# Attention, experts and FFN on one core: last tokens' products in float32, one addition on ScalarE, loads reordered

## The chip, the cores and the metric

One of the eight cores of a Trainium2 chip runs the whole kernel. The metric is the device time in microseconds (us); less is better. The trace names the engines PE (TensorE's matmuls), PEld (its weight loads), DVE (VectorE), ACT (ScalarE), POOL (GpSimd) and SP (the queue that issues most DMAs).

## The reference

Three layers follow one another on 2 sequences of 544 tokens (32 global, 512 local), 8 heads of 64:

```python
out_g = softmax(scale * q_g @ k_all.T) @ v_all            # global tokens see all
out_l = softmax(where(|i - j| <= 32, scale * q_l @ k_l.T, -1e9) ++ scale * q_l @ k_g.T) @ v   # local: window and globals
x = tokens(out)                                           # 1088 x 512
e = argmax(x @ w_gate); gate = softmax(...)[e]             # one of 8 experts per token
# each expert takes its first `capacity` = 288 tokens, in the tokens' order
y = relu(disp @ w1[e]) @ w2[e]                             # 512 -> 1024 -> 512
x = gate * y
h = x @ w_in; g = clip-like(h); out = g @ w_out            # 512 -> 2048 -> 512
```

Every softmax divides by its sum plus 1e-9.

## The kernel before, in words

The order of every engine is written out by hand; the engines run their instructions in that order and wait on semaphores.

**Attention** runs in 16 steps `k` (2 sequences x 2 pairs of token tiles x 4 pairs of heads). In the round of step `k` the program issues `exps(k+1)` (ScalarE), `scores(k+2)` (TensorE, then VectorE adds the mask, L313), the items of `first[k]`, `transp(k)` and its evacuation `evac_t(k)` (ScalarE and VectorE), `av(k-1)` (TensorE) with its evacuation by VectorE (L356), and the items of `plan[k]`. The four groups of global queries go through `glob1`, `glob1b`, `glob2`, `glob3`, one a step, beginning at steps 0, 3, 5 and 8. In PSUM the banks of kind "V" rotate, and `glob1` holds two of them until `glob1b`.

**Routing** of a pair of token tiles is put into three steps by `route(k, b, tp)`: at `k` the logits, `recips` (add 1e-9 to the sums of the softmax, then the reciprocal, both VectorE, L507 and L508) and `choose` (argmax and one-hot, L536); at `k+1` `slots` (each token's place in its expert, and the running counts `racc`) and the first `x_rows` (the token turned back to rows, scaled by the reciprocal); `scatter` puts the rows into the DRAM tensor `xd` by an indirect DMA of GpSimd. Routed steps are 7, 10 and 13; the last pair is routed behind step 15.

**Weights** of the experts come in chunks of 128x1024. `weight_load` issues the DMA on SP; `weight_h` (ScalarE, L218) writes the rounded half H; `weight_l` (L230) writes the rest L = raw - H. Products are taken as three of `float32r` (H x, L x, H x_low). The first eight chunks (units 0 and 1, expert 0) are loaded at steps 2 to 9, cast on ScalarE at steps 5 to 12, and their L's are GpSimd's. Raw buffers number four until the attention's memory is given up, then eight.

**The last two tiles** of tokens don't go through DRAM: `xt0` is loaded from `xd` once the earlier scatters have landed, and the last rows are added to it by a product with a matrix `place` that has a one at each token's slot. Their rows are split into halves first (L723 on ScalarE, L729 on VectorE), so that the products are five sets of four (L739). The sum is split again and is the first input of expert 0.

**The experts** follow: `expert_tile` runs 48 matmuls of 512 columns for up to 128 tokens; `rest` runs again for the tokens above 128 and above 256. The jobs in `todo` cast the next expert's chunks between them, one or two at each call of `bg` (ScalarE, every eighth on VectorE, L220), and take their L's on VectorE at the next call. Then comes the FFN.

Of the kernel before, what the change touches and what calls it, by code (L numbers as in the profile page):

```python
# [19 lines left out]
WARM_0, WARM_1, WARM_2, WARM_3, WARM_4 = 9, 5, 3, 2, 0  # L20
# [8 lines left out]
def tile_attention_moe_ffn(  # L29
# [97 lines left out]
    def load_values(u):  # L127
        b, hp = divmod(u, NHP)
        VT[u] = at.tile([P, 5, P], F32, tag="vt", name=f"vt{u}", bufs=NBU)
        nc.sync.dma_start(VT[u], vx[b, hp])  # L130
        if hp % 2 == 1:
            QG[u // 2] = at.tile([P, 4 * SG], F32, tag="qgt", name=f"qgt{u}", bufs=4)
            nc.sync.dma_start(QG[u // 2], qg[b, hp // 2])
# [29 lines left out]
    half = const.tile([P, 1], F32, name="half")  # L163
    racc = const.tile([P, E], BF16, name="racc")
# [29 lines left out]
    def raw_tile(name):  # L194
        n = nraw[0]
        nraw[0] += 1
        if more_raw and n % 8 >= 4:
            return more_raw[0].tile([P, 1024], F32, tag="raw2", name=name, bufs=4)
# [341 lines left out]
    def slots(b, lo, hi):  # L540
# [3 lines left out]
        for i in range(lo, hi):  # L544
# [11 lines left out]
            op=ALU.mult)  # L556
        rs = rt.tile([P, E], F32, tag="rs", name=f"rs{b}{lo}", bufs=1)
        nc.vector.tensor_reduce(out=rs, in_=OH[b][:, lo:hi, :].rearrange("p i e -> p e i"), op=ALU.add, axis=AX.X)
        with nc.allow_low_precision(reason="whole numbers, one of the terms not zero"):
            nc.vector.tensor_reduce(out=sidx[:, ts], in_=ex[:, :n, :], op=ALU.add, axis=AX.X)  # L560
# [40 lines left out]
    def consts():  # L601
        nc.gpsimd.tensor_copy(tri_b, tri_f)
        nc.gpsimd.memset(ones_b, 1.0)
        nc.gpsimd.memset(half, 0.5)
        nc.gpsimd.memset(racc, 0.0)
# [20 lines left out]
    def keep_warm(n):  # L626
        warm = ps_a("warm")
        for _ in range(n):
            nc.tensor.matmul(warm, zero.bitcast(BF16)[:, :P], zero.bitcast(BF16)[:, :512], start=True, stop=True)
# [13 lines left out]
    load_values(5)  # L643
    wq = [(u, c) for u in range(2) for c in range(4)]
# [3 lines left out]
    for g, k in enumerate((0, 3, 5, 8)):  # L648
# [10 lines left out]
    def route(k, b, tp):  # L659
# [19 lines left out]
    for k in range(NS):  # L679
# [54 lines left out]
    for ns, k0 in ((range(5), range(KD)),):  # L734
        for n in ns:
            x, at_ = parts[n]
            for k in k0:
                ks = slice(k * P, (k + 1) * P)
                nc.tensor.matmul(px0[:, ks], x[:, ks], at_, start=n == k == 0, stop=n == 4 and k == KD - 1)  # L739
# [11 lines left out]
    nc.vector.tensor_scalar(out=cnt, in0=pc[:1, :E], scalar1=float(cap), scalar2=None, op0=ALU.min)  # L751
    actx.close()
# [218 lines left out]
    for c in range(2):  # L971
        weight_load(3, c)
    XH[0, 0] = X0
    x_load(1, 0, 1)
    for c in range(2, 4):
        weight_load(3, c)
    wl = [(2 * e + i, c) for e in range(1, E) for i in range(2) for c in range(4)]
    wn = [8]
# [17 lines left out]
    todo = [(2 * e + i, c) for e in range(1, E) for i in range(2) for c in range(4)]  # L996
# [14 lines left out]
    for e in range(E):  # L1011
# [3 lines left out]
        def bg():  # L1015
# [11 lines left out]
            for f in wide[n] if wide else ():  # L1027
                f()
            if e > 0 and small:
# [381 lines left out]
```

## Time and profile before

| | us |
|---|---|
| median of 3 runs | 467.0 |
| lowest, highest run | 464.29, 467.17 |
| profiled execution, its own time | 462.71 |
| its span, first to last instruction | 460.8 |
| PE busy | 442.3 (96%) |
| PEld busy | 372.1 (81%) |
| DVE busy | 335.2 (73%) |
| ACT busy | 242.9 (53%) |
| POOL busy | 95.8 (21%) |

The granted TensorE clock is 1.00 (of 2.4 GHz) over the whole span. A busy share is an average over stages with different limits: attention and routing take the first 91 us, the experts the time to about 254, the FFN the rest. An instruction that stalls at its start still counts as busy on its engine, so that a longer duration than usual of the same form is a wait too.

### The profile page before, as it was taken

The numbers are of one execution on the slowest core, as the hardware profiler recorded it, in microseconds if no ns is written. First come the engines' busy times: TensorE is split into PE (matmuls) and PEld (weight loads), VectorE is DVE, ScalarE is ACT, GpSimd is POOL, SyncE is SP. The second block draws the span as 40 slices with busy tenths as digits, with TensorE's granted clock in tenths as the row PEclk, the third lists the DMA queues.
The fourth block names the chain that finished last, engine by engine and source line by source line (L and its number), as shares of the span: only waits on it lengthen the run. The fifth ranks groups of instructions, "written<-read, shape, count | busy, mean of one in ns | idle before, by whom it ended". The sixth has DMA issues, their size and how long they took to land. (4 is left out here: it accounts for less than half of the span.)

```text
span 460.8 us, 8110 instructions
## 1 busy us (share of the span) xinstructions
PE 442.3 (96%) x2875; PEld 372.1 (81%) x2876; DVE 335.2 (73%) x715; ACT 242.9 (53%) x508; POOL 95.8 (21%) x98
## 2 busy tenths in 40 slices
PE   8998989999999999999999899998999999999997
PEld 4876677787577777777777799998999899999996
DVE  4787798674156389936898976787888988878633
ACT  5779666273244478726766675645444344534321
POOL 1105365300000000000001642232133131322321
PEclk9999999999999999999999999999999999999999
DMA  8999554589349169963986340653221410000203
GB/s 273 312 332 366 171 185 134 192 278 395 129 127 316 47 242 389 375 239 123 341 299 243 98 149 0 211 200 93 91 75 64 134 49 1 0 2 0 70 1 127
DMA packets 34595, 79.17 MB, mean 172 GB/s; under 512 B 3761, under 2 KB 8497, under 8 KB 34546
## 3 DMA queue, kind: packets, MB, share of 16 engines
q1 hardware_dynamic: 31698, 70.40, 44.8%
q0 software_dynamic: 1408, 4.46, 2.9%
q10 hardware_dynamic: 1440, 3.67, 2.3%
q8 instruction: 29, 0.48, 0.5%
q14 instruction: 20, 0.16, 0.1%
HBM read 63.77 MB, written 14.75 MB: 170 GB/s over the span
## 5 line engine op out<-in xcount | busy, mean ns | idle before, releaser
L1158 PE MATMUL fh<-oldH,H 128*128 128x256 f32 (+1 forms) x256 | 64.7, 328 | 2.6 <-DVE g L1176 2.1
L230 DVE TENSOR_TENSOR L<-raw,H 128x1024 fp32r<-128x1024 f32 x56 | 66.3, 1217 | 0.9 <-ACT H L218 0.6
L1198 PE MATMUL acc<-oldH,H 128*128 128x256 f32 (+2 forms) x240 | 65.1, 332 | 1.3 <-ACT H L280 0.7
L218 ACT CAST H<-raw 128x1024 fp32r<-128x1024 f32 x57 | 58.0, 1049 | 10.0 <-PEq L895 8.2
L1158 PEld LDWEIGHTS fh<-oldH,H 128*128 128x128 f32 x256 | 44.8, 189 | 6.0 <-DVE g L1176 2.5
L1184 ACT CAST oldH<-g 128x256 fp32r<-128x256 f32 (+2 forms) x36 | 17.9, 496 | 56.8 <-DVE g L1176 56.8
L1198 PE MATMUL acc<-oldH,L 128*128 128x256 f32 (+2 forms) x144 | 47.2, 328 | 0.0
L1198 PEld LDWEIGHTS acc<-oldH,H 128*128 128x128 f32 x240 | 43.3, 189 | 4.0 <-issue 1.0
L1172 DVE SCALAR_TENSOR_TENSOR r<-r 128x256 f32<-128x256 f32 (+2 forms) x48 | 31.2, 650 | 21.0 <-ACT r L1163 21.0
L1185 POOL TENSOR_TENSOR oldH<-g,oldH 128x256 fp32r<-128x256 f32 (+2 forms) x24 | 26.8, 1119 | 73.3 <-ACT oldH L1184 63.5
L1158 PE MATMUL fh<-oldH,L 128*128 128x448 f32 (+1 forms) x128 | 41.6, 325 | 0.0
L599 DVE TENSOR_TENSOR hl<-pt,hh 128x512 fp32r<-128x512 f32 (+1 forms) x24 | 15.7, 653 | 35.6 <-ACT hh L598 35.6
L860 PE MATMUL py<-H,hh 128*128 128x512 f32 (+1 forms) x96 | 38.6, 402 | 0.0
L860 PE MATMUL py<-L,hh 128*128 128x512 f32 (+1 forms) x96 | 37.6, 391 | 0.0
L285 DVE TENSOR_TENSOR L<-co,H 128x512 fp32r<-128x512 f32 x32 | 22.9, 722 | 18.4 <-ACT H L280 18.4
L1163 ACT ACTIVATE r<-fh,half 128x256 f32<-128x256 f32 (+2 forms) x48 | 27.0, 564 | 17.5 <-PE fh L1158 17.1
L845 ACT ACTIVATE hs<-ph 128x512 f32<-128x512 f32 (+1 forms) x24 | 14.4, 598 | 41.2 <-PE ph L842 41.0
L1158 PE MATMUL fh<-oldL,H 128*128 128x384 f32 x128 | 35.2, 339 | 0.2
L931 POOL DMA_INDIRECT yg_own<-yd,idx x2 | 2.3, 1135 | 147.5 <-DVE co L270 147.2
L270 DVE SCALAR_TENSOR_TENSOR co<-raw,ca 128x512 uint32<-128x512 uint32 x32 | 31.5, 992 | 0.9
L324 ACT ACTIVATE sm<-sm,ng 128x224 f32<-128x224 f32 x64 | 30.0, 476 | 3.7 <-DVE ng L313 3.7
L860 PE MATMUL py<-H,hl 128*128 128x512 f32 (+1 forms) x96 | 28.5, 401 | 0.0
(202 smaller groups left out, 1014.8 us busy)
## 6 DMA issues: line engine op xcount, KB each, us to landing
raw<-in_w_dram SPq DMA_DIRECT2D x64, 512.0 KB, 5.7
raw<-in_w_in_dram SPq DMA_DIRECT2D x14, 512.0 KB, 4.9
raw<-in_w_out_dram SPq DMA_DIRECT2D x12, 512.0 KB, 3.7
xd<-zero SPq DMA_DIRECT2D x16, 256.0 KB, 5.9
vt<-in_vx_dram SPq DMA_DIRECT2D x8, 320.0 KB, 4.8
xt<-xd SPq DMA_DIRECT2D x8, 256.0 KB, 6.5
yd<-zero SPq DMA_DIRECT2D x8, 256.0 KB, 3.7
yd<-ys SPq DMA_DIRECT2D x8, 256.0 KB, 5.6
```

The lines of the kernel that those rows point to most:

```text
L218: nc.scalar.copy(dst, src)
L230: eng.tensor_tensor(out=L[:, sl], in0=RAW.pop((u, c)), in1=H[:, sl].bitcast(F32), op=ALU.subtract)
L270: nc.vector.scalar_tensor_tensor(out=o, in0=lo, scalar=29, in1=a, op0=ALU.logical_shift_right, op1=ALU.bitwise_or)
L285: nc.vector.tensor_tensor(out=L[:, sl], in0=CV.pop((g, c)), in1=H[:, sl].bitcast(F32), op=ALU.subtract)
L324: nc.scalar.activation(SM[s][:, c, :], SM[s][:, c, :], AF.Exp, bias=NG[s][:, c:c + 1], scale=-1.0, accum_out=SUM[b][:, i, col:col + 1])
L860: nc.tensor.matmul(py[:rows], h[:, 4 * q + k, :rows], w[:, 4 * q + k, :], start=q == i == 0, stop=q == 1 and i == len(terms) - 1)
L1158: nc.tensor.matmul(ph[:, :n], w[:, k, :], XC[c][i // 2][:, k, :], start=n_ == 0, stop=n_ == len(terms) - 1)
L1163: nc.scalar.activation(RS[f % 2][:, :n], ph[:, :n], AF.Relu, bias=half, scale=0.5)
L1172: nc.vector.scalar_tensor_tensor(out=r[:, :n], in0=r[:, :n], scalar=1.0, in1=r[:, :n], op0=ALU.min, op1=ALU.mult)
L1184: nc.scalar.copy(gh[:, :n], gt[:, :n])
L1185: nc.gpsimd.tensor_tensor(out=gl[:, :n], in0=gt[:, :n], in1=gh[:, :n].bitcast(F32), op=ALU.subtract)
L1198: nc.tensor.matmul(a[:, :n], p[:, ds], q, start=f == 0 and i == 0, stop=f == nfl - 1 and i == 2)
```

## The change

- `recips`: the addition of 1e-9 is a ScalarE activation (`Identity`, bias from a new constant tile `tiny`) instead of a VectorE `tensor_scalar`.
- `weight_h`/`weight_l` of the first eight chunks run at steps 5, 6, 8, 9, 11, 12, 14, 15 instead of 5 to 12. GpSimd does the L's of six; those of the last two are VectorE's, behind the first input's split.
- The fourth group of global queries is loaded behind unit 5 instead of unit 7, and its four parts run at steps 9 to 12 instead of 8 to 11.
- `slots` is cut in two: the running counts are their own function `counted`, issued behind the slots, at the end behind `place`.
- The last route that is scattered (step 13): both later tokens' rows and scatters come sooner, the third tile's at the head of step 15.
- Last tokens: no halves; `place` and the rows stay float32, and the products are three sets, with `xt0` first.
- Expert 1's first unit is loaded in two parts: two chunks ahead of `xt0`'s load, two by `next_w` in the first expert, behind the four of unit 3, which now come ahead of `x_load(1, 0, 1)`; the order of the `todo` jobs and the rotation of raw buffers follow.
- Warm-up matmuls: one more at the start, two fewer behind the slots.

```diff
-WARM_0, WARM_1, WARM_2, WARM_3, WARM_4 = 9, 5, 3, 2, 0
+WARM_0, WARM_1, WARM_2, WARM_3, WARM_4 = 10, 5, 1, 2, 0
...
+    def load_queries(g):
+        QG[g] = at.tile([P, 4 * SG], F32, tag="qgt", name=f"qgt{g}", bufs=4)
+        nc.sync.dma_start(QG[g], qg[divmod(2 * g, NHP)[0], 2 * g % NHP // 2])
...
-        if more_raw and n % 8 >= 4:
+        if more_raw and 2 <= n % 8 < 6:
...
-        nc.vector.tensor_scalar_add(sv, sv, 1e-9)
+        nc.scalar.activation(sv, sv, AF.Identity, bias=tiny)
         nc.vector.reciprocal(sv, sv)
...
+    def counted(b, lo, hi):
         rs = rt.tile([P, E], F32, tag="rs", name=f"rs{b}{lo}", bufs=1)
         nc.vector.tensor_reduce(out=rs, in_=OH[b][:, lo:hi, :].rearrange("p i e -> p e i"), op=ALU.add, axis=AX.X)
...
     load_values(5)
+    load_queries(3)
...
-    for g, k in enumerate((0, 3, 5, 8)):
+    for g, k in enumerate((0, 3, 5, 9)):
...
-        plan[k + 1] += [lambda: slots(b, lo, hi)] + x[1:2] + sc[:1]
-        plan[k + 2] += x[2:] + sc[1:]
-
+        plan[k + 1] += [lambda: slots(b, lo, hi), lambda: counted(b, lo, hi)]
+        if k + 2 < NS - 1:
+            plan[k + 1] += x[1:2] + sc[:1]
+            plan[k + 2] += x[2:] + sc[1:]
+        else:
+
+            plan[k + 1] += sc[:1] + x[1:2] + sc[1:2]
+            first[k + 2] += x[2:] + sc[2:]
+
+    conv_at = [5, 6, 8, 9, 11, 12, 14, 15]
...
-        if 5 <= k < 13:
-            c = k - 5
+
+        if k in conv_at:
+            c = conv_at.index(k)
             weight_h(*wq[c], nc.scalar)
-            weight_l(*wq[c], nc.gpsimd)
-    for c in range(4):
+            if c < 6:
+                weight_l(*wq[c], nc.gpsimd)
+    for c in range(2):
         weight_load(2, c)
...
-    halves = [[rt.tile([P, DM], F32R, name=f"late{i}{n}") for n in "hl"] for i in range(2)]
-    for (xa, _), x in zip(halves, late):
-        nc.scalar.copy(xa, x)
-    place = rt.tile([P, 2, P], F32R, name="place")
+    place = rt.tile([P, 2, P], F32, name="place")
...
-    for (xa, xb), x in zip(halves, late):
-        nc.vector.tensor_tensor(out=xb, in0=x, in1=xa.bitcast(F32), op=ALU.subtract)
+    counted(1, 3, NB_)
...
-    parts = [(halves[i][0], place[:, i, :]) for i in range(2)] + [(xt0, ident)]
-    parts += [(halves[i][1], place[:, i, :]) for i in range(2)]
...
+    for n, (x, at_) in enumerate([(xt0, ident), (late[0], place[:, 0, :]), (late[1], place[:, 1, :])]):
+        for k in range(KD):
+            ks = slice(k * P, (k + 1) * P)
+            nc.tensor.matmul(px0[:, ks], x[:, ks], at_, start=n == k == 0, stop=n == 2 and k == KD - 1)
...
+    for c in (6, 7):
+        weight_l(*wq[c], nc.vector)
     actx.close()
...
-    for c in range(2):
-        weight_load(3, c)
     XH[0, 0] = X0
+
+    wl = [(2 * e + i, c) for e in range(1, E) for i in range(2) for c in range(4)]
+    wl[2:8] = wl[4:8] + wl[2:4]
+    for c in range(4):
+        weight_load(3, c)
     x_load(1, 0, 1)
-    for c in range(2, 4):
-        weight_load(3, c)
...
-    wn = [8]
+    wn = [6]
...
-    todo = [(2 * e + i, c) for e in range(1, E) for i in range(2) for c in range(4)]
+    todo = list(wl)
...
+            if e == 0 and n in (4, 5):
+                next_w()
```

## Rows read from the trace of the kernel before

**Rows 1.** Stretches: busy PE, PEld, DVE, ACT, POOL; clock, DMA share, GB/s.
```profile
37.60:44.20 6.60, 4.63 (x52) 3.48 (x44) 6.46 (x28) 6.60 (x22) 4.14 (x2) 1.00 1.02 373
44.20:52.46 8.26, 7.32 (x107) 5.74 (x104) 5.13 (x20) 4.10 (x13) 0.64 (x2) 1.00 0.87 303
...
56.63:62.58 5.95, 4.38 (x46) 3.51 (x43) 5.88 (x17) 4.86 (x15) 5.44 (x4) 1.00 0.71 193
...
120.00:131.00 11.00, 11.00 (x53) 5.81 (x52) 1.81 (x5) 3.69 (x6) 0.00 (x0) 1.00 0.01 2
```

**Rows 2.** Waits of 37 to 92 us: total us, times, longest us.
```profile
PE sp L308 <- DVE m L532: 1.9, 1, 1.9
PE px L487 <- DVE xT L356: 1.6, 1, 1.6
...
PE g L367 <- DMA qgt<-in_qg_dram: 0.9, 1, 0.9
```

**Rows 3.** Order of time, VectorE around routing: start, us, line, operation, out<-in.
```profile
39.39 1.31 DVE L507 TENSOR_SCALAR ssum<-ssum 128x16 f32<-128x16 f32 x1
...
43.49 1.33 DVE L536 TENSOR_TENSOR oh<-iota_sb,i 128x24 bf16<-128x24 f32 x1
...
58.45 2.53 DVE L507 TENSOR_SCALAR ssum<-ssum 128x16 f32<-128x16 f32 x1
...
72.62 1.86 DVE L507 TENSOR_SCALAR ssum<-ssum 128x16 f32<-128x16 f32 x1
...
81.93 0.17 DVE L507 TENSOR_SCALAR ssum<-ssum 128x16 f32<-128x16 f32 x1
```

**Rows 4.** Order of time, GpSimd's L's in steps 10 and 13.
```profile
58.57 4.78 POOL L230 TENSOR_TENSOR L<-raw,H 128x1024 fp32r<-128x1024 f32 x2
...
72.05 2.39 POOL L230 TENSOR_TENSOR L<-raw,H 128x1024 fp32r<-128x1024 f32 x1
```

**Rows 5.** The load of unit 6's queries: its issue, and its landing.
```profile
L125 SPq DMA_DIRECT2D qr<-in_qd_dram x1: 733/733/733, 36.0 to 36.0; - x1
...
DMA to landing us min/median/max: 6.7/6.7/6.7
```

**Rows 6.** Order of time, ScalarE's small copies in steps 11 and 13.
```profile
66.30 0.21 ACT L424 COPY xTg<-gpv 128x64 f32<-128x64 f32 x1 [2.33 <-PE gpv L419]
...
72.52 0.44 ACT L455 COPY ls<-lt 128x256 f32<-128x256 f32 x2
```

**Rows 7.** Order of time, the last tokens' products.
```profile
85.02 0.33 SPq L714 DMA_DIRECT2D xt<-xd  x1
...
86.67 0.81 PE L629 MATMUL warm<-zero 128*128 128x512 bf16 x3
...
87.29 0.42 DVE L725 TENSOR_TENSOR place<-iota_sb,sidx 128x256 fp32r<-128x256 f32 x1
...
88.78 1.11 PE L739 MATMUL px<-ident,xt 128*128 128x128 f32 x8
...
90.11 0.61 PE L739 MATMUL px<-place,late1l 128*128 128x128 f32 x4
```

**Rows 8.** Order of time, VectorE in the first expert.
```profile
96.41 0.69 DVE L599 TENSOR_TENSOR hl<-pt,hh 128x512 fp32r<-128x512 f32 x1 [1.66 <-ACT hh L598]
...
98.15 0.69 DVE L220 CAST H<-raw 128x1024 fp32r<-128x1024 f32 x1
...
101.72 4.62 DVE L230 TENSOR_TENSOR L<-raw,H 128x1024 fp32r<-128x1024 f32 x4
```

**Rows 9.** Groups of instructions by line: busy us, mean ns.
```profile
L324 ACT ACT_TABLE_LOAD x1 | 1.3, 1283 | 1.7 <-PEq L1401 1.7
...
L391 DVE TENSOR_SCALAR pg<-pg,gs 128x576 f32<-128x576 f32 x4 | 2.1, 520 | 0.3
```

**Rows 10.** Order of time, TensorE's first warm-up.
```profile
1.31 3.88 PE L629 MATMUL warm<-zero 128*128 128x512 bf16 x9 [1.31 <-POOL zero L142]
```

**Rows 11.** Waits of 91 to 135 us: total us, times, longest us.
```profile
PEld ph L842 <- DVE xl L599: 0.5, 1, 0.5
```

More of the change, by code (lines that the diff above doesn't have):

```diff
@@ L130, in load_values @@
         nc.sync.dma_start(VT[u], vx[b, hp])
-        if hp % 2 == 1:
-            QG[u // 2] = at.tile([P, 4 * SG], F32, tag="qgt", name=f"qgt{u}", bufs=4)
-            nc.sync.dma_start(QG[u // 2], qg[b, hp // 2])
+        if hp % 2 == 1 and u // 2 not in QG:
+            load_queries(u // 2)
+    def load_queries(g):
+        QG[g] = at.tile([P, 4 * SG], F32, tag="qgt", name=f"qgt{g}", bufs=4)
+        nc.sync.dma_start(QG[g], qg[divmod(2 * g, NHP)[0], 2 * g % NHP // 2])
     mask_sb = at.tile([P, NLT, WIN], F32, name="mask_sb")
@@ L163, in tile_attention_moe_ffn @@
     half = const.tile([P, 1], F32, name="half")
+    tiny = const.tile([P, 1], F32, name="tiny")
     racc = const.tile([P, E], BF16, name="racc")
@@ L556, in slots @@
             op=ALU.mult)
+        with nc.allow_low_precision(reason="whole numbers, one of the terms not zero"):
+            nc.vector.tensor_reduce(out=sidx[:, ts], in_=ex[:, :n, :], op=ALU.add, axis=AX.X)
+    def counted(b, lo, hi):
         rs = rt.tile([P, E], F32, tag="rs", name=f"rs{b}{lo}", bufs=1)
         nc.vector.tensor_reduce(out=rs, in_=OH[b][:, lo:hi, :].rearrange("p i e -> p e i"), op=ALU.add, axis=AX.X)
-        with nc.allow_low_precision(reason="whole numbers, one of the terms not zero"):
-            nc.vector.tensor_reduce(out=sidx[:, ts], in_=ex[:, :n, :], op=ALU.add, axis=AX.X)
         nc.vector.tensor_tensor(out=racc, in0=racc, in1=rs, op=ALU.add)
@@ L604, in consts @@
         nc.gpsimd.memset(half, 0.5)
+        nc.gpsimd.memset(tiny, 1e-9)
         nc.gpsimd.memset(racc, 0.0)
@@ L623, in zero_fill, with keep_warm @@
             nc.sync.dma_start(yd[0:1, :], zero[:1, :])
-    def keep_warm(n):
+    def keep_warm(n, cols=512):
         warm = ps_a("warm")
         for _ in range(n):
-            nc.tensor.matmul(warm, zero.bitcast(BF16)[:, :P], zero.bitcast(BF16)[:, :512], start=True, stop=True)
+            nc.tensor.matmul(warm[:, :cols], zero.bitcast(BF16)[:, :P], zero.bitcast(BF16)[:, :cols], start=True,
+                             stop=True)
     keep_warm(WARM_0)
@@ L727, in tile_attention_moe_ffn @@
         in1=sidx[:, ntile - 2:].unsqueeze(2).to_broadcast([P, 2, P]), op=ALU.is_equal)
-    for (xa, xb), x in zip(halves, late):
-        nc.vector.tensor_tensor(out=xb, in0=x, in1=xa.bitcast(F32), op=ALU.subtract)
+    counted(1, 3, NB_)
     px0 = ps_t("px0")
     keep_warm(WARM_2)
-    parts = [(halves[i][0], place[:, i, :]) for i in range(2)] + [(xt0, ident)]
-    parts += [(halves[i][1], place[:, i, :]) for i in range(2)]
[L734 to L739, printed above, removed]
+    for n, (x, at_) in enumerate([(xt0, ident), (late[0], place[:, 0, :]), (late[1], place[:, 1, :])]):
+        for k in range(KD):
+            ks = slice(k * P, (k + 1) * P)
+            nc.tensor.matmul(px0[:, ks], x[:, ks], at_, start=n == k == 0, stop=n == 2 and k == KD - 1)
     keep_warm(WARM_3)
@@ L970, in tile_attention_moe_ffn @@
     vals = {}
-    for c in range(2):
+    XH[0, 0] = X0
+    wl = [(2 * e + i, c) for e in range(1, E) for i in range(2) for c in range(4)]
+    wl[2:8] = wl[4:8] + wl[2:4]
+    for c in range(4):
         weight_load(3, c)
-    XH[0, 0] = X0
     x_load(1, 0, 1)
-    for c in range(2, 4):
-        weight_load(3, c)
-    wl = [(2 * e + i, c) for e in range(1, E) for i in range(2) for c in range(4)]
-    wn = [8]
+    wn = [6]
     def next_w(eng=None):
```

## The prediction, made before the change was built

> **What bounds the kernel now.** I read the stretches first, to see which engine is full where. From the start of the experts on, TensorE is: in 120 to 131 us it is busy 11.00 of 11.00 us while the DMA share is 0.01 [rows 1]. That part the change hardly touches, so whatever is won ahead of the first expert's matmuls goes to the end one for one, unless the first expert is fed worse than before. The attention ahead of it is bound differently from step to step. In step 8 (44.20 to 52.46) TensorE is busy 7.32 of 8.26 us; in step 10 (56.63 to 62.58) it is VectorE, 5.88 of 5.95 us, with TensorE at 4.38 [rows 1].
>
> Second, the waits, to see which wait ends last in such a step. Three of TensorE's are over 0.9 us: 1.9 at the scores (L308), 1.6 at the turn of the first tokens (L487), 0.9 for the fourth group's queries [rows 2]. The first is put down to VectorE's maximum (L532), which those scores don't read. The queries of unit 6 that they do read were issued at 36.0 and landed 6.7 us later, at 42.7 [rows 5]; I take that as the true cause. So step 8 can't begin sooner, whatever is taken off VectorE in step 7.
>
> Third, the order of time on VectorE around routing. The addition of 1e-9 on 128x16 takes 0.17 us undisturbed but 1.31, 2.53 and 1.86 in the three routed steps; the one-hot comparison (L536) once takes 1.33 us [rows 3]. In both late cases GpSimd is in an L of a weight chunk: 58.57 for 4.78 (two in a row), 72.05 for 2.39, and VectorE goes on when one of these ends [rows 3, 4]. So VectorE stands still while GpSimd holds something that both need.
>
> **The change part by part.** All savings are on the clock of the old trace.
>
> *Queries earlier, fourth group one step later.* The 64 KB load goes from behind unit 7 to behind unit 5, ahead of unit 6's queries on SP's queue. The 0.9 us wait of step 8 [rows 2] goes: -0.9. Price of the move: what is queued behind it lands a little later; I estimate 0.17 us from the 373 GB/s that the full queue moves in step 7 [rows 1] (the bound is 0.33, one more issue on SP, as for L714 [rows 7]). The group's matmuls aren't saved, they come in step 9.
>
> *The addition on ScalarE.* Step 7: the add is gone from VectorE, but the scores of step 8 wait for their DMA anyway, so 1.31 - 0.17 is worth nothing. Step 10: the add is behind the copy of the logits and ready before VectorE comes to the reciprocal, so VectorE gets back 2.53 - 0.17 = 2.36. TensorE had waited 1.6 for it; beyond that TensorE is the bound: -1.6. Part of the rest is needed, since the fourth group's scaling (L391, 0.52 us [rows 9]) now falls into this step, in front of the choice, and can itself meet a GpSimd L. Step 13: here ScalarE runs full, and the add comes behind its copies of the logits, 72.52 + 0.44 [rows 6]. With 0.2 for the add, VectorE's reciprocal starts at about 73.2 instead of 72.62 + 1.86 = 74.5 [rows 3]: -1.3. Behind the waiting reciprocal stand the evacuation of the transposed weights and the choice, so this wait does not vanish, it is shorter. Fourth add: VectorE's 0.17 is saved beside other work, nothing.
>
> What an add costs ScalarE no row shows. The nearest is its 128x64 copy, 0.21 us [rows 6]; the upper bound is the 0.44 that two wider copies take together [rows 6]. I take 0.2, nearest in size, and only step 13 pays it: +0.2.
>
> The Trainium skill speaks against this edit: "ScalarE: Activation LUTs", section "Rules for kernel authors", sends additions to VectorE, and its section "What ACT_TABLE_LOAD costs" gives an ACTIVATE with a per-partition bias some 280 ns plus 0.833 ns a column, an estimate of 0.29 us here; the sum would be worse by 0.1. The trace agrees only for an undisturbed VectorE (0.17); beside a GpSimd L it does not.
>
> *GpSimd's L out of steps 7, 10, 13.* It works for the one-hot of step 7 (1.33, and undisturbed I put it at the add's 0.17 [rows 3]), which again is covered by the DMA wait. Two L's of 2.4 us (half of 4.78 [rows 4]) go to VectorE, behind the first rows.
>
> *The fourth group's last matmuls in step 12.* ScalarE copies their result and waited 2.33 us for it in step 11 [rows 6], where VectorE was late anyway. In step 12 nothing covers it: the exponentials, logits, the add and the evacuation that release steps 13 and 14 come behind it. Between nothing and 2.33 I take 1.4: ScalarE gets there some 0.9 us later than TensorE starts these matmuls. +1.4.
>
> Up to the last tokens: -0.9 + 0.17 - 1.6 - 1.3 + 0.2 + 1.4 = -2.0.
>
> *Last tokens.* The number of TensorE's instructions doesn't fall: three groups of float32 products are 3 x 8, the old ones 4 + 4 + 8 + 4 + 4, because the product with float32 `xt` already appears as 8 [rows 7]. What changes is the order: the 8 of `xt` no longer need `place`. The old chain: `place` ends at 87.29 + 0.42 = 87.71 and the last product at 90.11 + 0.61 = 90.72 [rows 7]. New: one warm-up of 0.27 behind 86.67, 8 instructions at 0.12 (from 1.11 for 8, the overlap of the last taken off) to 87.9, then 16 to 89.9: -0.8. This holds if `xt` lands before. It was issued at 85.02 [rows 7] and used at 88.78 without a wait; now the last scatter ahead of it is one turn earlier and two weight loads fewer stand before it. The ScalarE and VectorE halves that go away were beside or behind this. Counting moved behind `place` saves a tenth.
>
> *First expert.* VectorE gets the two L's, 2.3 us by half of 4.62 [rows 8], in front of its own. It stood idle 1.66 us before the first `hl` [rows 8], which takes most of that. But the cast of a chunk (0.69) leaves this early gap and comes behind four L's (4.62) that run right up to the split of the second rows [rows 8], for which TensorE waits 0.5 us already [rows 11]. So +0.7 (bounds 0 and 2.3 + 0.7 = 3.0).
>
> *Warm-ups.* The first gets one more, 3.88 / 9 = 0.43 us [rows 10]. The start shifts by that, and the 1.9 us DMA wait of step 8 takes it up: nothing (0.43 without that wait).
>
> Sum: -2.0 - 0.8 - 0.1 + 0.7 = -2.2, which I round to -2 for the many small waits left out. The profiled execution ran 462.7 us, about 1.9 more than its span, so it would be 460.7. It is 4.3 faster than the median of the runs shown, 467.0; with the same difference I forecast **465.0 us**.
>
> **Rivals.**
> - *It adds up.* If nothing is paid back, the stalls beyond 0.17 (1.14 + 1.16 + 2.36 + 1.69 = 6.3 [rows 3]) plus 0.9 and 0.8 give -8, 459. For it: VectorE is full in step 10. Against: two of the four stalls lie under the DMA wait. With half of that, -5, it passes 1%: 462. Chance 0.18.
> - *It moves only.* VectorE waits for ScalarE's add instead of GpSimd, the fourth group's late matmuls cost their full 2.33, and the first expert 1.5 of its 3.0: -0.3, 466.7. For it: in step 13 ScalarE has no pause. Chance 0.22.
> - *Slower: the first expert is fed late.* Two of unit 2's chunks are loaded only behind the first L's, and ScalarE's cast of them stands in order ahead of the split of the second rows. If they land late, ScalarE stands and TensorE behind it, 1 us for 1 us; beyond 2 us the whole gain is gone, at 5 us late it is 470. Against: the four loads ahead of them, 2 MB, take 5.6 us at 373 GB/s [rows 1], and the casts come later than that, behind the first L's and the whole first half of the expert; the DMA share of 0.01 at 120 to 131 says that nothing is short later. Chance 0.05.
> - *Another table.* If the add needs a table other than the exponentials', each change is 1.28 us [rows 9]; two for each of the first three adds are 7.7 us: 472.7. Against: copies, casts and exponentials share the one load of the whole execution. Chance 0.02.
>
> **How the numbers follow.** The forecast has the remaining 0.53, with its own bounds 463 to 466.5. The range takes in half of "it adds up" and all of "it moves only" with the spread of the runs shown (464.29 to 467.17): 461.3 to 467.9. A measurement can tell about 1% (4.7 us) from no change. Faster by that: 0.18, nearly all of it "it adds up"; slower by that: 0.05, the last two; same 0.77.
>
> **What would show it.** The new profile should have reciprocals of 0.25 us with no long 128x16 addition on VectorE; no wait for the queries; `px` ending about 2 to 3 us sooner with `xt` ahead of `place`; a wait of 1 to 2 us of ScalarE for the group's result, now in step 12; and VectorE without a gap in the first expert, TensorE waiting some 1 us for the second rows' split. Wrong I am if step 8 begins before 42.7 (then it was VectorE, not DMA), if ScalarE loads a second table, or if casts in the first expert wait for DMA.

## The result, and the profile after

The kernel after takes 469.7 us (median of 8 executions, 466.8 to 472.83), the kernel before 465.57 (8 executions, 463.85 to 467.17): ratio 1.0085, 95% interval 1.0056 to 1.0113. The forecast was 465.0, in a range of 461.3 to 467.9. The change costs about 4 us where 2 were to be won. The profiled execution of the kernel after ran 469.87 us (span 468.1), 7.2 more than that of before (462.71).

First the terms of the prediction. These rows of the kernel after, in order of time (start, us, engine, line, operation, in brackets the idle time before it and what ended it), answer to [rows 3] and [rows 6]:

```profile
41.02 0.25 DVE L512 RECIPROCAL ssum<-ssum 128x16 f32<-128x16 f32 x1 [1.11 <-ACT ssum L511]
43.78 0.18 DVE L540 TENSOR_TENSOR oh<-iota_sb,i 128x24 bf16<-128x24 f32 x1
56.56 0.31 ACT L511 ACTIVATE ssum<-ssum,tiny 128x16 f32<-128x16 f32 x1
57.05 0.25 DVE L512 RECIPROCAL ssum<-ssum 128x16 f32<-128x16 f32 x1
71.28 0.21 ACT L428 COPY xTg<-gpv 128x64 f32<-128x64 f32 x1 [2.82 <-PE gpv L423]
74.80 0.26 DVE L512 RECIPROCAL ssum<-ssum 128x16 f32<-128x16 f32 x1 [1.14 <-ACT ssum L511]
```

The long additions are gone, the one-hot comparison takes 0.18 instead of 1.33, ScalarE's add takes 0.31, and ScalarE waits 2.82 for the group's result in step 12.

The last tokens, which answer to [rows 7]; the product with `xt` comes ahead of `place`:

```profile
88.29 1.05 PE L749 MATMUL px<-ident,xt 128*128 128x128 f32 x8
88.69 0.42 DVE L740 TENSOR_TENSOR place<-iota_sb,sidx 128x256 f32<-128x256 f32 x1
89.18 2.04 PE L749 MATMUL px<-place,xr 128*128 128x128 f32 x16
91.80 0.48 PE L854 MATMUL ph<-H,x0h 128*128 128x512 f32 x1
```

The last row is the experts' first matmul: 91.80, where the kernel before had it at 91.32. The forecast had it 2.9 us sooner (2.0 up to the last tokens, 0.8 and 0.1 in them). Where that went is seen in the stretches (columns as in [rows 1]; the third figure from the end is the granted clock):

```profile
48.00:50.00 2.00, 2.00 (x12) 1.42 (x11) 1.22 (x5) 1.90 (x9) 0.70 (x1) 0.57 0.92 349
50.00:52.00 2.00, 2.00 (x12) 1.52 (x10) 1.33 (x8) 0.52 (x2) 1.96 (x2) 0.58 0.34 107
...
64.00:66.00 2.00, 1.64 (x13) 1.33 (x14) 1.81 (x8) 2.00 (x9) 0.80 (x1) 0.83 0.00 0
66.00:68.00 2.00, 2.00 (x10) 1.42 (x9) 1.24 (x7) 0.24 (x3) 1.98 (x2) 0.50 0.34 131
...
96.00:98.00 2.00, 0.00 (x0) 0.00 (x0) 1.23 (x2) 0.00 (x1) 0.00 (x0) 1.00 0.81 316
98.00:100.00 2.00, 1.35 (x7) 1.21 (x8) 0.00 (x0) 2.00 (x4) 0.98 (x2) 0.87 0.51 114
100.00:102.00 2.00, 2.00 (x6) 1.51 (x6) 1.95 (x3) 0.96 (x2) 0.00 (x0) 0.50 0.64 195
102.00:104.00 2.00, 2.00 (x9) 1.54 (x8) 1.00 (x1) 1.43 (x2) 0.00 (x0) 0.78 0.69 185
```

Three times TensorE's clock is at or near half, that is at its lower level of 1.2 GHz. The profiled execution of before had 1.00 throughout. As an estimate, what is lost is at most the stretch times what is missing to 1: 0.86 + 0.84 in 48 to 52, 0.34 + 1.00 in 64 to 68 and 0.4 in the next 2 us (0.81), together 3.4 us ahead of the experts. Without them the first matmul would stand at 88.4, 2.9 sooner than before. So the sum of the terms up to there came out, though not each of them (see below), and by this estimate a clock that the prediction didn't speak of took it all. e3's profiled execution, below, agrees: at the full clock, with two fillers of 0.8 us more, its first matmul is at 89.43.

The bigger part comes behind. TensorE is idle from 96 to 98. These rows (SP's issues, GpSimd's last scatter, and the first expert's first Relu on ScalarE) show why:

```profile
88.43 1.92 SPq L209 DMA_DIRECT2D raw<-in_w_dram  x4
90.26 0.98 POOL L572 DMA_INDIRECT xd<-xr,sidx  x1 [0.30 <-issue]
97.96 0.34 SPq L790 DMA_DIRECT2D xt<-xd  x1
98.00 0.60 ACT L857 ACTIVATE hs<-ph 128x512 f32<-128x512 f32 x1 [4.19 <-DVE L L234]
```

The load of the next rows (`xt`) has to wait until the last scatter has landed, and it is issued at 97.96; the Relu starts at the same moment, 4.19 us after ScalarE was free. In the kernel before the same rows stand so:

```profile
87.04 0.89 SPq L205 DMA_DIRECT2D raw<-in_w_dram  x2
90.06 0.97 POOL L566 DMA_INDIRECT xd<-xr,sidx  x1 [0.30 <-issue]
93.88 0.34 SPq L778 DMA_DIRECT2D xt<-xd  x1
94.36 0.60 ACT L845 ACTIVATE hs<-ph 128x512 f32<-128x512 f32 x1 [1.06 <-PE ph L842]
```

There the Relu waits for its own matmuls only (1.06). The Relu doesn't read `xt`. Both wait for the scatter: e9's trace, below, names it as what ends the Relu's wait. I take it that `hs`, which the Relu writes, has memory that held the attention's rows, which the scatter reads; the traces show the wait, not the addresses. Then the clock falls, for another 1.7 us (98 to 104).

So the difference of 7.2 us: 0.5 at the first matmul, 3.2 more at the first Relu, 1.7 of clock behind it. In the rest of the first expert TensorE waits 0.24 for `xh`, as in before, and 0.75 for `xl`, the low half of the second rows; what is left, about 1 us, stays open.

### The profile page after: what moved, and what is told of

Its sections match the earlier page's. It is cut to its first block, busy times and chain, and to the rows that moved or that the text cites. A ratio compares the mean times of both kernels' runs of the same rounds, so it can differ in the third digit from the quotient of the medians.

```text
span 468.1 us, 8101 instructions
## 1 busy us (share of the span) xinstructions
PE 448.4 (96%) x2874; PEld 376.1 (80%) x2875; DVE 330.4 (71%) x711; ACT 242.5 (52%) x510; POOL 90.5 (19%) x97
## 5 line engine op out<-in xcount | busy, mean ns | idle before, releaser
L234 DVE TENSOR_TENSOR L<-raw,H 128x1024 fp32r<-128x1024 f32 x58 | 68.6, 1217 | 0.7 <-ACT H L222 0.4
L317 DVE CUSTOM_DVE_ANT_0 sm<-sp,mask_sb 128x224 f32<-128x224 f32 x64 | 21.0, 386 | 12.3 <-PE sp L312 10.8
```

What stands on the lines that cost most here:

```text
L234: eng.tensor_tensor(out=L[:, sl], in0=RAW.pop((u, c)), in1=H[:, sl].bitcast(F32), op=ALU.subtract)
L317: nc.vector.tensor_tensor_reduce(out=SM[s][:, c, :], in0=sp[h][:, t * WIN:(t + 1) * WIN], in1=mask_sb[:, 2 * tp + t, :], op0=ALU.add, op1= ...
```

## The experiments

All ratios are against the kernel before, timed on the same chip. "First matmul" and "first Relu" are those of the first expert, in the profiled execution of the kernel; in before they are at 91.32 and 94.36. The theories at the start: (1) the four loads of unit 3 ahead of the next rows' load hold up the scatters; (2) the two L's that VectorE makes there hold up the Relu.

**e1_loads: two of the four loads back behind the next rows' load.**

```
-    for c in range(4):
+    for c in range(2):
         weight_load(3, c)
     x_load(1, 0, 1)
+    for c in range(2, 4):
+        weight_load(3, c)
```

> Undoes one part: two of unit 3's four loads go behind the load of expert 1's rows again. Theory 1 (loads in front): in the changed kernel 2 MB of weights are issued at 88.43 to 90.35, just ahead of the last two scatters (88.93, 90.26); these land only at about 97.9, and the first Relu of the experts (L857), whose buffer lies where the scattered rows lay, waits 4.2 us for them. With two loads fewer ahead the scatters land at about 94, the Relu begins at 94 to 95.5, TensorE has no 3 us gap, its clock stays at 1.00 from 98 to 104, and the run takes 464 to 466. Theory 2 (L's in front): VectorE's four L's in a row (92.62 to 97.23) hold up the scatters' descriptors on GpSimd. Then the Relu stays at about 98 and the time at about 469.

Measured: 465.95 us, ratio 1.0015 (0.9979 to 1.005). Of SP and ScalarE:

```profile
87.06 0.89 SPq L209 DMA_DIRECT2D raw<-in_w_dram  x2
93.59 0.34 SPq L790 DMA_DIRECT2D xt<-xd  x1
94.01 0.60 ACT L857 ACTIVATE hs<-ph 128x512 f32<-128x512 f32 x1 [1.08 <-PE ph L854]
```

The Relu now waits for its own matmuls only, and it begins while VectorE's four L's still run in a row (from 91.74, 4.61 us). Theory 1 holds.

**e2_l_on_gpsimd: the last two L's on GpSimd.**

```
     for c in (6, 7):
-        weight_l(*wq[c], nc.vector)
+        weight_l(*wq[c], nc.gpsimd)
```

> The changed kernel with the two L's of chunks 6 and 7 on GpSimd behind the scatters, in place of VectorE; the four loads stay in front. Theory 2 (L's in front): VectorE has only two L's ahead of the first hl, the scatters land by about 95, and the Relu begins at 95 to 96; 3 us faster than the changed kernel. Theory 1 (loads in front): the scatters still land at about 97 to 98 and the Relu waits 3.5 to 4.5 us; time 469 within 1.

Measured: 468.83 us, ratio 1.009 (1.0051 to 1.0129). The Relu waits as before:

```profile
84.08 1.92 SPq L209 DMA_DIRECT2D raw<-in_w_dram  x4
94.17 0.34 SPq L790 DMA_DIRECT2D xt<-xd  x1
94.21 0.60 ACT L857 ACTIVATE hs<-ph 128x512 f32<-128x512 f32 x1 [4.21 <-DVE L L234]
```

This speaks against theory 2, but not by itself: beside GpSimd's two L's the two that VectorE keeps take 5.37 us (from 89.09), so VectorE isn't free sooner. What settles it is e1, where the L's stay and the wait goes, and e5, next, where VectorE has only two L's, done at 95.74, and the Relu still waits to 98.15. The name of the releaser, an L of VectorE, misleads here as it did in the kernel after.

**e5_before_loads4: the four loads alone, on the kernel before.**

```
-    for c in range(2):
+    for c in range(4):
         weight_load(3, c)
     XH[0, 0] = X0
     x_load(1, 0, 1)
-    for c in range(2, 4):
-        weight_load(3, c)
```

> The kernel before with one edit: all four loads of unit 3's weights stand ahead of the load of the next rows, as in the kernel after. Theory 1 (the loads just ahead of the scatters delay the scattered rows): the load of the next rows moves from 93.88 to about 97.5, the first expert's first Relu, which follows it, waits 4 us, and the time rises by 2 to 4 us (ratio 1.004 to 1.009), with no change up to the experts' first matmul at 91.3. Rival (the loads hurt only together with the kernel after's earlier or later instructions, its VectorE L's or its swapped buffers): Relu without a wait above 1.5 us, ratio within 0.003 of 1.

Measured: 468.89 us, ratio 1.0092 (1.0061 to 1.0124): this one edit costs as much as the whole change.

```profile
88.04 1.92 SPq L205 DMA_DIRECT2D raw<-in_w_dram  x4
98.11 0.34 SPq L778 DMA_DIRECT2D xt<-xd  x1
98.15 0.60 ACT L845 ACTIVATE hs<-ph 128x512 f32<-128x512 f32 x1 [3.85 <-issue]
```

**e3_warm: three matmuls of 512 columns on zeros ahead of the places in steps 8 and 11.**

```
     conv_at = [5, 6, 8, 9, 11, 12, 14, 15]
+    plan[8].append(lambda: keep_warm(3))
+    plan[11].append(lambda: keep_warm(3))
```

> The changed kernel with three dense matmuls of 512 columns put ahead of the slots in step 8 and step 11, where TensorE has only products of 32 and 8 columns or waits. Theory 3 (clock): TensorE fell to the lower clock at about 48.5 and 65 because its work just before was thin; with the filler the granted clock is 1.00 from 44 to 72, the scores and transposes of steps 9 and 12 take 2.0 us in place of 3.5, and the experts begin about 1.7 us sooner (3.0 won, 1.3 paid for the filler): 467 to 468.5. Rival: these stretches lie beside ScalarE's and VectorE's work; then the clock is 1.00 but the experts begin no sooner than 91.3.

Measured: 471.26 us, ratio 1.0144 (1.0069 to 1.022). The profiled execution, 465.99 us, had the full clock everywhere, its first matmul at 89.43 (2.4 us sooner than the kernel after) and its first Relu, held up by 4.43 us, at 95.86. The other three took 470.33 to 472.8, at mean clocks of 0.989 to 0.993. That trace agrees with the account of the clock, the median doesn't bear it out, and what those three executions lost stays open.

**e4_group_step8: group 4's work back in steps 8 to 11.**

```
-    for g, k in enumerate((0, 3, 5, 9)):
+    for g, k in enumerate((0, 3, 5, 8)):
```

> Undoes one part: the fourth group of global queries runs at steps 8 to 11 again, its queries still loaded early. Theory 3 (clock): the group's sixteen products of 256 and 288 columns stand between the narrow products and the slots again, so the clock stays at 1.00 in 48 to 52; 1 to 2.5 us faster than the changed kernel, the fall at 65 may stay. Rival (the forecast's step): the move to step 9 itself was worth 0.9 us, and taking it back makes the run 0.5 to 1 us slower.

Measured: 466.03 us, ratio 1.0016 (0.998 to 1.0052), 3.2 us better than the kernel after. The profiled execution was the slowest of the ten (470.5, clock 0.985, half clock in 44 to 48 and 98 to 104), so its trace shows the clock's cost rather than what the edit saves; its Relu still waits 4.50 us.

**e6_loads_and_group: e1 and e4 together.**

> The kernel after with the edits of e1_loads and e4_group_step8 together. If the two losses are apart (the rows late in the first expert, and group 4's work in step 9 instead of 8), the gains add up: e1 gave 3.3 us and e4 gave 3.0 us against the kernel after's ratio of 1.0085, so 463.0 us, ratio 0.995. Rival (both edits only spare the same low clock in the first expert): no more than the better of them, ratio 1.001, 465.5 us.

Measured: 464.41 us, ratio 1.0 (0.9981 to 1.0019): by the ratios 0.7 us below either, not 3. In the first expert ScalarE waits for weights; the view of its waits in 90 to 112 us (total, times, longest) has

```profile
ACT H L222 <- DMA raw<-in_w_dram: 3.0, 3, 1.2
```

No such wait stands in the kernel before's view of that stretch. These are unit 2's last chunks, which the change loads behind unit 3's.

**e7_before_add: only the add on ScalarE, on the kernel before.**

```
+    tiny = const.tile([P, 1], F32, name="tiny")
...
-        nc.vector.tensor_scalar_add(sv, sv, 1e-9)
+        nc.scalar.activation(sv, sv, AF.Identity, bias=tiny)
```

> The kernel before with the addition of 1e-9 on ScalarE and nothing else. By the prediction's step: 1.6 us at the reciprocals of step 10 and 1.3 at step 13 go from the routing, less 0.3 for ScalarE's add: last tokens about 2 us sooner, 463 us, ratio 0.994 to 0.997. Rival (time saved in the attention is taken again before the experts begin, by the clock or by the scatters): the experts' first matmul moves by under 0.7 us and the ratio lies within 0.003 of 1.

Measured: 462.93 us, ratio 0.9962 (0.9939 to 0.9985), 1.8 us of the forecast terms' 2.7 (1.6 + 1.3 - 0.2). The profiled execution had a low clock in 48 to 60 (0.79, 0.50, 0.85), so its own first matmul (93.47) says nothing.

**e8_before_late: only the last tokens' float32 products, on the kernel before.**

```
-    parts = [(halves[i][0], place[:, i, :]) for i in range(2)] + [(xt0, ident)]
-    parts += [(halves[i][1], place[:, i, :]) for i in range(2)]
...
+    for n, (x, at_) in enumerate([(xt0, ident), (late[0], place[:, 0, :]), (late[1], place[:, 1, :])]):
```

> The kernel before with its last tokens by three float32 products of two passes (no split in two float32r parts, one warm-up instead of three, the counting left where it was). By the prediction's step: 0.8 us less between the last scores and the experts' first matmul, ratio about 0.998. Rival (nothing, since TensorE's passes are 24 in both and the chain is that of the places): first matmul of the experts within 0.3 us of 91.3.

The warm-ups behind the slots go from three to one as well. Measured: 464.6 us, ratio 1.0002 (0.998 to 1.0023): nothing. One of its ten executions took 1482.78 us and isn't counted in the ratio. From the end of the slots (`sidx`) to the first matmul it is 3.95 us here (88.34 to 92.29), 4.24 in before (87.08 to 91.32), 3.32 in the kernel after (88.48 to 91.80). Why it is so little here stands in TensorE's rows:

```profile
88.77 1.16 PE L730 MATMUL px<-ident,xt 128*128 128x128 f32 x8 [0.46 <-DMA xt<-xd]
```

The product that now comes first waits for its load. In the kernel after a scatter stands one turn earlier and the load is there in time.

**e9_weights_before: the kernel after with all that concerns weights as in before** (H and L in steps 5 to 12, every L on GpSimd, four loads of unit 2 in the attention, two of unit 3 ahead of the next rows and two behind).

```
-        if k in conv_at:
-            c = conv_at.index(k)
+        if 5 <= k < 13:
+            c = k - 5
             weight_h(*wq[c], nc.scalar)
-            if c < 6:
-                weight_l(*wq[c], nc.gpsimd)
-    for c in range(2):
+            weight_l(*wq[c], nc.gpsimd)
+    for c in range(4):
         weight_load(2, c)
...
-    wl[2:8] = wl[4:8] + wl[2:4]
```

> The kernel after with all that concerns the weights put back as it was before: the H and L of units 0 and 1 in steps 5 to 12 with every L on GpSimd, four loads of unit 2 in the attention, two loads of unit 3 ahead of the next rows' load and two behind. What stays of the change: the add on ScalarE, the queries early, group 4's work one step later, the last tokens' float32 products. Theory 3 (the whole loss of the kernel after is in the order of the weights: four loads ahead of the scatters, and unit 2's last chunks late, on which casts in the first expert waited 3 us in e6): the add's gain of e7 shows, 462.0 to 463.5 us, ratio 0.994 to 0.997. Rival (GpSimd's L's back in the routing steps stall VectorE again by 1.3 to 1.9 us each, and this is what e6 gained and lost): ratio 0.999 or more.

Measured: 466.72 us, ratio 1.0047 (1.0021 to 1.0074). Theory 3, that all of the loss is in the weights, falls. Two views of it say more than the rest together. ScalarE's first Relu:

```profile
95.97 0.60 ACT L853 ACTIVATE hs<-ph 128x512 f32<-128x512 f32 x1 [2.50 <-DMA xd<-xr,sidx]
```

Here the wait is put down to the scatter itself. And TensorE in step 11:

```profile
63.26 0.16 PE L551 MATMUL pc<-base_b,ones_b 1*128 1x8 bf16 x1 [1.51 <-DVE xr L505]
...
64.78 1.86 PE L312 MATMUL sp<-kr,qr 64*128 64x224 f32 x8
```

It waits 1.51 us for VectorE's rows with nothing else to do; the scores behind that take 1.86 us instead of 1.03, at a clock of 0.50 in 66 to 68.

**e10_weights_and_group: e9 with group 4 back in steps 8 to 11.**

> As e9_weights_before, with group 4's work back at steps 8 to 11. By the prediction's step (group 4 in step 12 costs 1.4 us): ratio 0.003 below that of e9, 0.991 to 0.994, about 461.5 us. Rival (its place is worth nothing that lasts to the experts, as e6 against e1 gave 0.0015 with intervals that overlap): within 0.001 of e9.

Measured: 462.77 us, ratio 0.995 (0.9929 to 0.997), 0.0097 below e9: 4.5 us from moving one group by a step. The group's 40 narrow products (1.67 us from 61.98) fill the place where e9 idles, and the clock is 1.00 through all the stretches of the attention. The first Relu still waits:

```profile
85.11 0.89 SPq L209 DMA_DIRECT2D raw<-in_w_dram  x2
92.35 0.34 SPq L786 DMA_DIRECT2D xt<-xd  x1
92.39 0.60 ACT L853 ACTIVATE hs<-ph 128x512 f32<-128x512 f32 x1 [1.92 <-DVE L L234]
```

**e11_add_and_queries: the kernel before with the add on ScalarE and the queries' load moved up.** e7's diff and

```
...
     load_values(5)
+    load_queries(3)
```

> The kernel before with two edits: 1e-9 added on ScalarE (e7, ratio 0.9962) and the last queries' load moved up to follow the values of unit 5. By the prediction's step the queries give another 0.7 us: ratio 0.9947, 462.2 us. Rival (the loads that the queries push back start step 8 later by as much as the wait that goes): 0.996 to 0.997, the same as e7.

Measured: 460.85 us, ratio 0.9925 (0.9897 to 0.9953). This is the fastest kernel here, below both. In its profiled execution (460.4 us, clock 1.00) step 8's scores wait for their queries, the first matmul comes 3.3 us sooner than in before, and the Relu doesn't wait for scatters:

```profile
42.09 1.03 PE L312 MATMUL sp<-kr,qr 64*128 64x224 f32 x8 [0.97 <-DMA qr<-in_qd_dram]
...
88.03 0.47 PE L848 MATMUL ph<-H,x0h 128*128 128x512 f32 x1
...
91.12 0.60 ACT L851 ACTIVATE hs<-ph 128x512 f32<-128x512 f32 x1 [1.11 <-PE ph L848]
```

The forecast for these two parts alone was 0.9 - 0.17 + 1.6 + 1.3 - 0.2 = 3.4.

**e12_l_spaced: e10 with the L's out of the routing steps, all on GpSimd.**

```
-        if 5 <= k < 13:
-            c = k - 5
+        if k in conv_at:
+            c = conv_at.index(k)
             weight_h(*wq[c], nc.scalar)
             weight_l(*wq[c], nc.gpsimd)
```

> As e10_weights_and_group, but with the H and L of units 0 and 1 in steps 5, 6, 8, 9, 11, 12, 14 and 15, as in the kernel after, and all eight L's on GpSimd. If taking GpSimd's L's out of the routing steps saves VectorE's stalls: 1 to 2 us below e10. Rival (the last two loads of unit 2 wait for the L's of steps 14 and 15, whose buffers they take, and so are issued close ahead of the scatters): the next rows' load lands later, first Relu waits over 1.5 us, ratio 1.002 or more.

Measured: 467.96 us, ratio 1.0075 (1.0048 to 1.0102). The time is the rival's, and so is its cause (unit 2's last loads wait for the last L's), but not the place: the Relu doesn't wait, the load of the last tokens' `xt` does. It stands on SP behind unit 2's last load, which waits for GpSimd's last L, is issued at 85.91 instead of 82.02 in e10, and TensorE waits for it:

```profile
90.52 2.08 PE L748 MATMUL px<-ident,xt 128*128 128x128 f32 x8 [4.97 <-DMA xt<-xd]
```

This is also why the change gives two L's to VectorE behind the first rows, and why unit 2's last two chunks have to be loaded later: these L's free the buffers that the loads take.

**e13_group_alone and e17_group_on_before: group 4 in steps 9 to 12, on e11 and on the kernel before.** The reverse of e4's diff.

> e11_add_and_queries with one edit more: group 4's work in steps 9 to 12 instead of 8 to 11, as in the kernel after. Theory 4 (in step 11 nothing is left for TensorE while VectorE finishes x rows, it idles about 1.5 us, and its clock falls behind that): the experts' first matmul 3 us later than in e11 (91 instead of 88.0), ratio 0.998 to 1.000. By the prediction's own term (1.4 us): 0.9955. Rival (the 3.7 us between e9 and e10 came with their other edits): under 0.002 above e11's 0.9925.

> The kernel before with one edit: group 4's work in steps 9 to 12 instead of 8 to 11. Theory 4 (in step 11 TensorE has nothing left while VectorE finishes x rows): a wait for xr of about 1.5 us ahead of the places of step 10's block, the experts' first matmul 1.5 to 3 us later than before's 91.3 in an execution without low clock, ratio 1.004 to 1.009. By the prediction's term: 1.4 us, 1.003. Rival (no cost without the kernel after's other edits): ratio within 0.002 of 1.

Measured: 472.98 us, ratio 1.0193 (1.0151 to 1.0235), and 471.58 us, ratio 1.0151 (1.0125 to 1.0177). Both profiled executions wait for VectorE's rows in step 11, 1.56 and 2.31 us, and their first matmul comes 1.75 us later than in e11 (89.78) and 1.98 later than in before (93.30). The rest of the loss lies elsewhere. In e13, and in e17 alike, TensorE stops at a branch of a later expert (a row of each):

```profile
239.98 0.71 PE L848 MATMUL ph<-H,x0h 128*128 128x512 f32 x1 [5.21 <-PEq L901]
```

```profile
242.77 0.77 PE L842 MATMUL ph<-H,x0h 128*128 128x512 f32 x1 [4.87 <-PEq L895]
```

In all the other traces, that of the kernel after among them, the longest such wait is 0.5 us. So these two runs show the idle time of step 11 again, and 1.75 to 2 us for the group's place ahead of the experts (e17's with a clock of 0.84 in 60 to 70); their ratios can't be read for it. There are four executions of each, and e13's spread from 467.99 to 475.1.

**e14_loads_behind, e15_after_loads_behind, e16_best_tried: all four loads of unit 3 behind the next rows' load**, on e10 (shown), on the kernel after, and on e11 with e8's edit.

```
-    for c in range(2):
-        weight_load(3, c)
     x_load(1, 0, 1)
-    for c in range(2, 4):
+    for c in range(4):
         weight_load(3, c)
```

> e10_weights_and_group with all four loads of unit 3 behind the next rows' load instead of two ahead and two behind. Theory 1, sharpened (the scattered rows land when the loads in front have drained): the next rows' load is issued about 3 us after the last scatter begins instead of 5.4, the first Relu's wait of 1.9 us goes, ratio 0.991, 461 us. Rival (the loads are needed where they stood): casts of unit 3 wait for DMA in the first expert and take back the 1.9 us, ratio 0.995 or more.

> The kernel after with the next rows' load ahead of all four loads of unit 3. Theory 1: first Relu without a wait above 1.2 us, as in e1; with group 4 in step 9 and unit 2's last chunks late the rest of e1's loss stays, ratio 0.999 to 1.002. Rival (loads that come later are late for the casts): ratio 1.004 or more, with ScalarE waiting for raw weights over 3 us in the first expert.

> e11_add_and_queries with the last tokens' float32 products and all four loads of unit 3 behind the next rows' load. Theory 1 says that the float32 products gave nothing in e8 because the scattered rows' landing hung on the loads, not on the last tokens: with the loads behind, their 0.8 us show, ratio 0.9907, 460.0 us. Rival (unit 3's weights come late): above e11's 0.9925.

Measured: 462.01 us, ratio 0.995 (0.993 to 0.9969); 468.34 us, 1.009 (1.0055 to 1.0126); 462.79 us, 0.9951 (0.9925 to 0.9978). In all three the next rows' load is issued 3.0 us after the last scatter begins and the Relu waits for its matmuls only (1.08 us). e14:

```profile
85.84 0.98 POOL L572 DMA_INDIRECT xd<-xr,sidx  x1 [0.30 <-issue]
...
88.83 0.33 SPq L786 DMA_DIRECT2D xt<-xd  x1
```

The mechanism is as theory 1 has it, but the time doesn't follow. e15 pays the 4 us at the casts instead:

```profile
97.49 1.05 ACT L222 CAST H<-raw 128x1024 fp32r<-128x1024 f32 x1 [2.22 <-DMA raw<-in_w_dram]
```

(and 0.73 to 0.79 at the next three, 4.5 in all), its rival's case. In e16 the product with `xt` waits 0.67 us for its load, as in e8, so the float32 products give nothing again. e14 has no such wait for `xt`, and one of 0.4 us at a cast; its executions at a mean clock of 0.999 or more took 460.0 to 461.77, those of e10 at 1.0 460.96 to 463.16. A gain, if there is one, is too small for these runs.

## Why the prediction was wrong

**The step that failed is the term for the first expert.** It had +0.7 us, with bounds of 0 and 3.0, for VectorE's L's alone, and put the scatters' wait at nothing. In the kernel after the first Relu waits 3.1 us longer than in before (4.19 instead of 1.06), for the scatters behind the four loads, and the clock takes an estimated 1.7 us more behind that.

**The rival that was written off came near, in another place.** "The first expert is fed late" looked for late weights at ScalarE's casts; in the kernel after no cast of the first expert waits for DMA. It argued that the four loads, 2 MB, take 5.6 us and nobody needs them sooner. It didn't ask what moves behind them. The time from the issue of the loads to that of the next rows' load, which waits for the scatters' landing:

| loads of unit 3 just ahead | kernels | us |
|---|---|---|
| two | before, e1, e6, e7, e8, e11, e13, e17 | 6.5 to 6.9 |
| two | e10, e9 | 7.2, 7.8 |
| four | after; e2 to e5 | 9.5; 10.1 to 10.2 |

With two loads it is about 6.8, although the last scatter begins 1.8 to 3.0 us after them (in e12, where it begins 6.2 us after them, it lands within 2.9); with four it is some 3 us more, and the extra 1 MB at the 373 GB/s of [rows 1] takes 2.8. The view of the DMA queues, taken in stretches of 0.5 us, shows both parts. In the kernel after the scatters' queue (software_dynamic) moves its first data in 93.5 to 94, at least 4.6 us after the first of the two scatters began (88.93); by then the loads have moved about 1 MB. Then the two queues share the engines (0.37 MB of scattered rows and 0.42 of loads in 94 to 96), and the last rows pass at about 97. In before the first data come in 91 to 91.5, 2.5 us after the first scatter began (88.52), and the rest moves to 93 with little beside it (0.14 MB of loads in 91 to 92). In e14, with no loads in front, they come 1.5 us after it began (86 and 84.51). Why the loads hold back the first data stays open.

In the kernel before this was already just in time: next rows' load at 93.88, first Relu at 94.36. Two more loads moved the landing by 4.1 us. The prediction's price for the case, 1 us for 1 us, was if anything low: in e5 the Relu waits 2.8 us longer (3.85 instead of 1.06) and the ratio gives 4.3 us, the fall of the clock behind the wait (0.85 in 96 to 100, 0.73 in 100 to 104) among them. Its chance of 0.05 was too small. The casts that it did look at waited too, 3.0 us in e6, a smaller loss of the same kind: e6 and e10 differ in the weights alone, 0.005 or 2.3 us.

**This bound also eats gains.** In e10 the products end sooner behind the slots than in e11 (3.32 us from `sidx` to the first matmul against 4.24), but the loads are issued closer to the scatters (1.8 us ahead of the last instead of 3.0) and the Relu waits 1.9 us. The term of 0.8 for the last tokens was right (0.92), and worth nothing while the scatters set the Relu; with `xt` late, as in e8 and e16, 0.3 and 0.1 us of it are left. "This holds if `xt` lands before" was the right condition to name.

**Group 4's place.** The term was +1.4, for ScalarE's wait in step 12 (2.82 instead of the 2.33 assumed as an upper end). The larger cost lay where the work was taken away: step 11, where it had filled TensorE's time while VectorE finished its rows. There e9, e13 and e17 idle 1.5 to 2.3 us, and the first matmul comes 1.75 us later in e13, at a full clock, and 3.0 us between e9 and e10, with the clock's fall. The prediction said of the old place only that VectorE was late there anyway; that is what made the filler useful. In the kernel after the L's stand elsewhere, VectorE is sooner and the wait is 0.78. What the group's place costs there stays open: e6 and e1, which differ in it alone, are 0.0015 apart, but so differ e4 and the kernel after, and these are 0.0069 apart (3.2 us). Undoing the loads (e1) or the group's place (e4) each takes back most of the loss, and both together (e6) hardly more, so the 4 us can't be divided between the two.

**The clock.** It was left out. The profiled execution of before, at 1.00 throughout, is an exception: of 35 executions of that kernel timed beside e5 to e8, 32 had a mean clock of 0.991 to 0.996 and took 463.15 to 467.11 us, the three at 0.999 and more 461.99 to 464.59 (of all 114 timed beside the experiments, 13 are at 0.999 and more). Those of the kernel after have 0.987 to 0.999. In e10 the six executions at 1.0 have a median of 461.3, the six at 0.996 of 463.3. So some 2 us of a median are clock, and taking the same distance between profile and median for both kernels was a guess. That distance, 4.3 us, also came from three runs with a median of 467.0; all eight have 465.57 and give 2.9, with which the same terms make 463.6 and the miss 6 us rather than 5.

The kernel after has a fall behind the idle time ahead of the Relu, and two in the attention. Ahead of 48 us TensorE had done 40 products of 32 columns and then some dozen of 8:

```profile
45.17 1.66 PE L423 MATMUL gpv<-gT,vt 128*64 128x32 f32 x40
46.76 0.17 PE L551 MATMUL pc<-base_b,ones_b 1*128 1x8 bf16 x1
...
47.84 0.71 PE L491 MATMUL px<-ident,xT 128*128 128x128 f32 x4
48.48 1.86 PE L312 MATMUL sp<-kr,qr 64*128 64x224 f32 x8
```

TensorE is counted busy throughout, and the clock falls. Ahead of the other, at 65, it had waited 0.78 and 0.36 us. That the narrow work is the cause is argued from this and from e3's profiled execution, not shown: e3's median went the other way.

Nor is a fall in these steps the kernel after's own. In the profiled executions of e5, e7 and e8 the clock falls to 0.50 between 48 and 51, behind a wait of TensorE for the fourth group's queries of 1.37, 1.91 and 1.57 us; in that of before this wait is 0.94 and the clock stays at 1.00. Loading the queries sooner takes the wait away, and five of e11's six executions have a clock of 0.999 or more. A wait doesn't always bring a fall, though: e13 waits 1.56 in step 11 and keeps 1.00. So part of what e11 gains over e7 (0.0037, 1.7 us where the term had 0.9 - 0.17) may be clock; no run separates it.

**What was right.** The sum for the add and the queries: 3.3 us at the first matmul of e11 against 3.4 forecast, 3.5 by its ratio. That it fits so well is partly luck: 0.8 of the 3.3 come from step 8, which begins at 42.09 instead of 42.90 and which the forecast held fixed. VectorE's stalls, which went with the add and the L's, and the order of the last tokens came as told; by itself the add of e7 gave 1.8 of its 2.7. ScalarE's add took 0.31 us where the text assumed 0.2. From the Trainium skill, "ScalarE: Activation LUTs", section "What ACT_TABLE_LOAD costs", the estimate was 0.29; the trace agrees to 0.02.

**"Wrong if step 8 begins before 42.7".** It began at 41.86 in the kernel after and at 42.09 in e11. In e11 its wait of 0.97 is put down to the queries' DMA, so there the DMA does set it. But the landing is no fixed point: issued 0.6 us later than in before (36.60 instead of 36.02), the queries were there 0.6 us sooner (by 42.09 instead of 42.7). In the kernel after the wait is 0.20 and put down to VectorE.

## What to carry to other kernels

Loads that aren't needed soon still cost time when they are issued just ahead of a transfer that is waited for, even one of another queue: look at what moves next behind them, and at everything that reuses the memory which that transfer reads. Before filler work is moved out of a step, look at what the engine would do there without it. And when the profiled execution has a full clock and the median lies 4 us above it, the clock belongs in the sum: time several executions and compare those with the same mean clock.

## What the runs showed of the hardware

- A scatter of one tile began at 90.06 in before, two loads of 0.5 MB being issued from 3.0 us ahead of it, and had landed by 93.88; with four such loads, from 1.8 us ahead, 7.7 us passed (90.26 to 97.96 in the kernel after); with none, 3.0 (e14). Its data move late behind the loads and then share the engines with them.
- The granted clock falls in an engine that shows no gap: 0.57 behind 2.7 us of products 32 and 8 columns wide. Each of the three falls in the kernel after cost about 1.7 us, by an estimate from the stretches. In e5, e7 and e8 it fell behind waits of 1.37 to 1.91 us; in e13 it stayed at 1.00 behind one of 1.56.
- A reordering in the attention (e13, e17; as many instructions on TensorE as before, within one) brought a stop of 4.9 to 5.2 us at a branch some 175 us later, where other kernels wait 0.5 at most. The profile's view of DMA queues lists a queue for instructions, which moves one or two transfers there (0.02 to 0.03 MB in 236 to 243) while the weight loads keep the engines busy; in before it moves one there too, and nothing stops. Whether the stop is a late transfer of instructions stays open.
